# Attention on TensorE's tiles: the second half's outputs turned by 64 partitions, scores in 64x32 tiles ahead of the products within, routing groups one tile sooner

## The chip, the cores and the metric

The kernel runs on one core of a Trainium2 chip. The metric is device time in microseconds (us). TensorE (PE in the rows, PEld its weight loads) does the matmuls, VectorE (DVE), ScalarE (ACT) and GpSimd (POOL) the elementwise work, and SP issues most transfers. Each engine takes its own instructions in order.

## The reference

Three stages, in float32. First a linear attention with decay over 4 batches, 8 heads, 768 tokens, head size 32 and state size 16: within a chunk, `M = (C B^T) * L` with `L[i,j] = exp(cum_i - cum_j)` for `i >= j`, and

```
y      = M x + (C state) * exp(cum)
state  = exp(sum la) * state + sum_j B_j x_j exp(cum_last - cum_j)
```

The outputs become 3072 rows of 256. Then a mixture of 8 experts, each row to the one with the largest `x @ w_gate` (two layers of 1024 hidden units, weighted by the softmax of the gate). Then a second mixture of 4 experts, in which each row goes through all, weighted by given probabilities.

## The kernel before, in words

The attention works on 24 tiles (u) of 128 tokens, six to a batch, each in two halves (k) of 64 tokens. One loop, `for i in range(NU + 1)`, runs all stages of neighbouring tiles against each other; in it the order on every engine is the order of the calls. A turn i does, for TensorE in this order before the change:

- `scores(i+1)`: C B^T, four matmuls of 64 rows and 64 columns of weights (tile position (64q, 64k)), 256 columns each, into the PSUM tile `cb`; VectorE then multiplies by `Lt` to make `M` (L501, L503).
- `stage_c(i-1)`: two matmuls with the output `yT` of a tile as weights and a constant `rhsT` as moving operand, which is an identity with the 8 gate columns beside it. They transpose the tile back to tokens and give the gate's logits at once (L573). `store` copies both out by ScalarE (`lg`, `xo`), and SP stores `xo` to the rows `xs`.
- `decay(i+2)`: one matmul of 512 columns into `abc`, of which VectorE's scan makes `Lt` (L477, L480). In seven turns `decays_c` follows, which makes the decays of three tiles (L459).
- `within(i)`: M x, 16 matmuls in 64x32 tiles at (64k, 32h), for head pair h and half k, into `y[32h.., k]` (L515).
- `across(i)`: C state, in 32x32 tiles at (r, r) for both halves, added into the same `y` (L527). The first tile of each batch has no state for its first half. ScalarE then copies `y` to `yT` (L533).
- `gain(i+1)`: 16 matmuls of 128 rows and 32 columns into `U` (L548), of which VectorE's scan `state` makes S (L557) at the start of the next turn.

GpSimd makes `br` (`decayed_b`) and `Cs` (`decayed_c`), and splits the first expert's weights (L166). Each fp32 matmul leaves two records in the trace.

The routing of the first mixture is done in three groups of tiles, `ENDS = (12, 18, 23)`: when the turn behind a group's last tile ends, `route` puts a list of small operations into `queue`, and `slot` takes up to six of them in a turn. They find the largest logit, rank the rows by matmuls with ones and build one-hot blocks (L236) of four tiles each to invert the order. Behind the first group (EARLY) two gathers of rows for the first expert are issued, so that its first products (`ahead`) can follow the loop; the last group is routed behind the loop. `DECAYS` says in which turn each `decays_c` stands.

Of the kernel before, what the change touches and what calls it, by code (L numbers as in the profile page):

```python
# [8 lines left out]
F32 = mybir.dt.float32  # L9
# [10 lines left out]
P = 128  # L20
NB, H, S, HD, DS = 4, 8, 768, 32, 16
NT = NB * S
NCH = S // P
L = 64
NU = NT // P
D = H * HD
E1, E2, F = 8, 4, 1024
# [3 lines left out]
CAP = max(CAPS)  # L31
CAP0 = 256
GAP0 = 152
EARLY = 12
ENDS = (12, 18, 23)
NSL = 512
NC = E1 * NSL // P + 1
BIG = 3 << 29
# [5 lines left out]
def body(tc, I, out):  # L44
    nc = tc.nc
    with ExitStack() as outer:
# [266 lines left out]
        with ExitStack() as ctx:  # L313
# [98 lines left out]
            nc.gpsimd.memset(brs[0], 0.0)  # L412
            nc.vector.memset(d1, 0.0)
            nc.vector.memset(pfg[0], 0.0)
            rhsT = [ac.tile([P, P + E1], F32, name=f"rhsT{k}") for k in range(2)]
            for k in range(2):
                nc.gpsimd.tensor_copy(rhsT[k][:, (0, E1)[k]:(P, E1 + P)[k]], ident)
            select(0)
            nc.scalar.copy(delta, selF[:, None, :].broadcast_to([P, H, L]))
            select_heads(0)  # L420
# [72 lines left out]
            def scores(u):  # L493
                BT, cm = cz[u // 3 % NBC][:, 2], BC[u // 3]
                Lt = LM[u]
                M = LM[u] = sp.tile([P, H, L], F32, tag="M", name="M", bufs=2)
                cb = pa.tile([P, 2, 512], F32, tag="cb", name="cb")
                for q, k in ((0, 0), (1, 1), (0, 1), (1, 0)):
                    r = slice(64 * q, 64 * q + 64)
                    ts = slice(u % 3 * P + k * L, u % 3 * P + k * L + L)  # L500
                    nc.tensor.matmul(cb[k * L:k * L + L, q, :4 * L], BT[r, ts], cm[r, :, ts], start=True, stop=True,  # L501
                                     tile_position=(64 * q, k * L), skip_group_check=True)
                nc.vector.tensor_mul(M.rearrange("p (q h) i -> p q (h i)", q=2), cb[:, :, :4 * L],  # L503
                                     Lt.rearrange("p (q h) i -> p q (h i)", q=2))

            def within(u, q):
                b, c = divmod(u, NCH)
                if q == 0:
                    LM[u, "y"] = pa.tile([P, 2, 512], F32, tag="y", name="y", bufs=1)
                y = LM[u, "y"]  # L510
                M = LM[u]
                for h in range(4):
                    for k in range(2):
                        r = slice(k * L, k * L + L)
                        nc.tensor.matmul(y[32 * h:32 * h + 32, k, q * L:q * L + L],  # L515
                                         xb[u % NXB][r, k, (2 * h + q) * HD:(2 * h + q + 1) * HD],
                                         M[r, 2 * h + q], start=(q == 0), stop=(c == 0 and k == 0),
                                         tile_position=(k * L, 32 * h), skip_group_check=True)

            def across(u):  # L520

                b, c = divmod(u, NCH)
                LM.pop(u)
                for k in range(2):
                    if c > 0 or k > 0:
                        for r in range(0, P, 32):
                            nc.tensor.matmul(LM[u, "y"][r:r + 32, k, :P], LM[u, "S"][r:r + 32, :, k],  # L527
                                             LM[u, "Cs"][r:r + 32, :, k * L:k * L + L],
                                             start=False, stop=True, tile_position=(r, r), skip_group_check=True)

            def copy_y(u):
                yT = LM[u, "yT"] = sp.tile([P, 2, P], F32, tag="yT", name="yT")
# [3 lines left out]
            def carry(u):  # L536

                U = LM[u, "U"] = pp.tile([P, HD, 3], F32, tag="oneA", name="U")
                nc.scalar.copy(U[:, :, 0], LM[u - 1, "S"][:, :, 2] if u % NCH else zero.bitcast(F32).broadcast_to([P, HD]))
# [19 lines left out]
            def decayed_c(u):  # L559

                Cs = sp.tile([P, 2, P], F32, tag="Cs", name="Cs", bufs=2)
                nc.gpsimd.tensor_mul(Cs, cz[u // 3 % NBC][:, :2, u % 3 * P:u % 3 * P + P],
                                     PF[u // 3][:, u % 3, None, :].broadcast_to([P, 2, P]))
                LM[u, "Cs"] = Cs

            def stage_c(u):

                yT = LM.pop((u, "yT"))
                tp = pa.tile([P, 2, P + E1], F32, tag="tp", name="tp")

                flat = tp.rearrange("p k c -> p (k c)")
                for k in range(2):
                    nc.tensor.matmul(flat[:, k * P:k * P + P + E1], yT[:, k, :], rhsT[k], start=(k == 0), stop=True,  # L573
                                     skip_group_check=True)
                LM[u, "tp"] = tp

            def store(u):
# [66 lines left out]
            bc_part(2 * P, HB)  # L644
            bc_next = load_bc(1)
            bc_next[0]()
            for k in range(2):
                nc.sync.dma_start(rhsT[k][:, (P, 0)[k]:(P + E1, E1)[k]], I["wg"][k])
            load(2)
            dpr = ac.tile([P, NU, E2], F32, name="dpr")  # L650

# [39 lines left out]
            def has(u):  # L691
                return 0 <= u < NU
# [39 lines left out]
            CASTS = {**dict.fromkeys((7, 9, 11, 13, 15, 16, 17, 18, 22, 23), 1), 19: 2, 20: 2, 21: 2}  # L732
            asks = [f for t in TILES for f in load_w(0, *t, pieces=4)]
            splits = list(TILES)
            DECAYS = {max(3 * m - 2 - 2 * (m > 5), 2): m for m in range(1, NU // 3)}
            CHUNKS = {0: 3, 1: 4, 2: 2, 3: 5}
            for i in range(NU + 1):
                if i % 2 == 0 and has(i + 4):
                    load(i + 4)
                if i in stage:  # L740
                    bc = load_bc(stage[i])
                    bc[0]()
                    for k in range(2):
                        heads[3 * stage[i] - 4 + k] = [lambda h=h, bc=bc: bc[1](h) for h in range(2 * k, 2 * k + 2)]
                for f in asks[:ASKS.get(i, 0)]:
                    f()
                asks = asks[ASKS.get(i, 0):]
                if i == 6:
                    nc.sync.dma_start(dpr, I["dp"].rearrange("p (u e) -> p u e", u=NU))
                if i == 9:  # L750
                    queue += probs
                for _ in range(CASTS.get(i, 0)):
                    if not ws:
                        ws = split_w(0, *splits.pop(0), 4)
                    steps_w += [ws[:2]]
                    ws = ws[2:]
                if has(i):
                    state(i)
                slot()
                if has(i + 1):  # L760
                    if i:
                        decayed_b(i + 1)
                    scores(i + 1)
                    carry(i + 1)
                for f in soon.get(i, ()):
                    f()
                if has(i - 1):
                    stage_c(i - 1)
                slot()
                if has(i + 2):  # L770
                    decay(i + 2)
                if i in CHUNKS:
                    chunks[CHUNKS[i]]()
                if i in DECAYS:
                    decays_c(DECAYS[i])
                if has(i + 1):
                    decayed_c(i + 1)
                for fs in steps_w:
                    for f in fs:
                        f()  # L780
                steps_w = []
                if 5 <= i < 8:
                    (counts, places_first, sums_of_ones)[i - 5]()
                for f in gathers[:1]:
                    if f:
                        f()
                gathers = gathers[1:]
                slot(2)
                if i in (3, 7, 11):
                    select_heads(i // 4 + 1)  # L790
                if i % 2 == 0 and has(i + 4):
                    select(i + 4)
                if has(i - 1):
                    store(i - 1)
                if has(i):
                    within(i, 0)
                    within(i, 1)
                    across(i)
                    copy_y(i)
                for f in heads.pop(i, ()):  # L800
                    f()
                if i < 2:
                    nc.gpsimd.memset(pfg[i + 2], 0.0)
                    blank(i + 4)
                slot(2)
                if has(i + 1):
                    gain(i + 1)
                if i - 1 in GROUPS and i < NU:
                    between, after = early() if i - 1 == EARLY else ((), ())
                    queue += route(*GROUPS[i - 1], psum_a, between)  # L810
                    if after:
                        queue.append(lambda after=after: gathers.extend(after))
# [572 lines left out]
def lay_out(x, a, B, C, moe_w_gate, moe_w1, moe_w2, moe2_domain_probs, moe2_w1, moe2_w2):  # L1385
# [11 lines left out]
    au = f(a.reshape(NB, H, NCH, 2, L).transpose(0, 2, 3, 1, 4)).reshape(2 * NU, H * L)  # L1397
    au = np.concatenate([au, au[:L - 2 * NU]], 0)
    d["au"] = np.concatenate([au, au], 0)
    d["wg"] = f(moe_w_gate.reshape(4, 2, HD, E1).transpose(1, 0, 2, 3)).reshape(2, P, E1)  # L1400
    d["w1"] = f(moe_w1.reshape(E1, 4, 2, HD, F).transpose(0, 2, 1, 3, 4)).reshape(E1, D, F)
    d["w2"] = f(moe_w2)
    v1 = moe2_w1.reshape(E2, 2, P, 2, 4, P).transpose(0, 4, 2, 1, 3, 5)
# [19 lines left out]
```

## Time and profile before

| | before |
|---|---|
| three timed runs, median | 770.13 us (769.84 to 770.41) |
| the profiled execution | 769.49 us, its span 767.8 us |
| TensorE, busy | 749.9 us, 98% of the span |
| VectorE | 557.1 us, 73% |
| ScalarE | 415.2 us, 54% |
| GpSimd | 471.4 us, 61% |

The profile shows one execution. The span runs from the first to the last instruction that it records. Busy times of TensorE are of pipelined matmuls whose ends are modelled, so on TensorE the starts say more than the durations.

### The profile page before, as it was taken

To read this page: it belongs to the slowest core of one execution; us is meant where nothing else is said; L and a number is where in the kernel's file an instruction comes from. 1 tells how busy PE (TensorE), PEld (TensorE's weight loads), DVE (VectorE), ACT (ScalarE), POOL (GpSimd) and SP (SyncE) were. 2 spreads that over 40 slices of the span, in tenths; PEclk is the share of its full clock that TensorE was granted. 3 is DMA by queue.
4 is the path that set the end of the run, shared out by engine and by line. 5 is a ranking of instruction groups with operands and counts; after the bars stand their busy time and mean duration, and the time that the engine had idled before them with its cause. 6 is when DMAs were issued, how large, how long until landed. Compare 5 with 4: busy or idle time off the path is not lost.

```text
span 767.8 us, 16862 instructions
## 1 busy us (share of the span) xinstructions
PE 749.9 (98%) x6510; PEld 710.8 (93%) x6510; DVE 557.1 (73%) x988; ACT 415.2 (54%) x931; POOL 471.4 (61%) x558
## 2 busy tenths in 40 slices
PE   8999899999999999999999999999999999999994
PEld 6666798999999999999999999999999999999994
DVE  8789845664467886787966779777687887868752
ACT  7776454545455555466564555555555565454540
POOL 5557767558762854587753558765366775465544
PEclk9999999999999999999999999999999999999998
DMA  7665355434423200010000001100000100000001
GB/s 210 172 192 152 90 180 163 134 118 133 134 74 98 55 2 2 1 28 29 28 28 1 2 1 51 32 14 16 1 2 29 29 1 1 7 36 17 26 28 56
DMA packets 36146, 45.57 MB, mean 59 GB/s; under 512 B 4512, under 2 KB 26016, under 8 KB 36064
## 3 DMA queue, kind: packets, MB, share of 16 engines
q1 hardware_dynamic: 31648, 36.29, 15.9%
q0 software_dynamic: 3360, 7.13, 2.9%
q8 instruction: 52, 0.85, 0.5%
q10 hardware_dynamic: 1056, 1.05, 0.5%
q14 instruction: 30, 0.25, 0.1%
HBM read 38.12 MB, written 6.34 MB: 58 GB/s over the span
## 4 chain that ended last, share of the span: by engine, by line
PE 65%; ACT 1%; DVE 0%; POOL 0%; issue 0%; POOLq 0%; ACTq 0%; DVEq 0%
PE po L1308 35%; PE x L1242 9%; PE z L1242 9%; PE w L1242 8%; PE y L1242 4%; ACT xc L865 0%; POOL out L1328 0%; ACT s L1255 0%; DVE h L1251 0%; PE poA L1308 0%; POOLq L1419 0%; ACT h L1248 0%; DVE c L1270 0%; DVE u L1263 0%; DVE acc L1318 0%
## 5 line engine op out<-in xcount | busy, mean ns | idle before, releaser
L1308 PE MATMUL po<-w,h 128*128 128x256 f32 x2280 | 280.1, 281 | 0.3 <-DVE h L1251 0.3
L1308 PEld LDWEIGHTS po<-w,h 128*128 128x128 f32 x2280 | 277.6, 188 | 0.5 <-DVE h L1251 0.5
L1248 ACT ACTIVATE h<-c 128x384 fp32r<-128x384 f32 x192 | 98.6, 525 | 149.8 <-DVE c L1282 80.5
L1261 POOL TENSOR_TENSOR g<-s,s 128x384 f32<-128x384 f32 x64 | 65.9, 1029 | 148.2 <-ACT s L1260 147.3
L1251 DVE SCALAR_TENSOR_TENSOR h<-c,h 128x384 fp32r<-128x384 f32 x192 | 145.6, 768 | 10.9
L1263 DVE TENSOR_TENSOR u<-y,s 128x384 f32<-128x384 f32 x64 | 35.5, 555 | 68.6 <-ACT s L1260 67.0
L166 POOL TENSOR_TENSOR wl<-raw,wh 128x256 fp32r<-128x256 f32 x72 | 55.5, 798 | 36.8 <-ACT wh L160 34.3
L1242 PE MATMUL x<-xc,wh 128*128 128x384 f32 x256 | 66.9, 342 | 1.3 <-ACT s L1255 0.6
L1242 PE MATMUL w<-xc,wh 128*128 128x384 f32 x256 | 65.5, 337 | 0.0
L1242 PE MATMUL z<-xc,wh 128*128 128x384 f32 x256 | 65.4, 336 | 0.0
L1282 DVE TENSOR_TENSOR c<-u,g 128x384 f32<-128x384 f32 x63 | 58.8, 933 | 0.0
L1255 ACT COPY s<-x 128x384 f32<-128x384 f32 x64 | 30.6, 479 | 50.8 <-PE x L1242 50.8
L904 ACT ACTIVATE hh<-ph 128x216 fp32r<-128x216 f32 (+8 forms) x69 | 33.4, 489 | 43.9 <-PE ph L274 38.6
L866 POOL TENSOR_TENSOR xc<-x,xc 128x384 fp32r<-128x384 f32 x28 | 32.7, 1166 | 37.0 <-ACT xc L865 36.8
L1251 DVE SCALAR_TENSOR_TENSOR h<-x,h 128x384 fp32r<-128x384 f32 x64 | 35.7, 558 | 24.2 <-ACT h L1248 23.9
L866 POOL TENSOR_TENSOR xc<-ts,xc 128x384 fp32r<-128x384 f32 x46 | 52.3, 1151 | 0.0
L906 DVE SCALAR_TENSOR_TENSOR hl<-ph,hh 128x216 fp32r<-128x216 f32 (+8 forms) x69 | 37.2, 549 | 16.9 <-ACT hh L904 16.3
L274 PE MATMUL ph<-xh,wh 128*128 128x480 f32 (+8 forms) x142 | 48.7, 343 | 0.4 <-DVE hl L906 0.4
L925 PE MATMUL po<-hh,wh 128*128 128x480 f32 (+8 forms) x142 | 48.3, 340 | 0.0
L274 PE MATMUL ph<-xh,wl 128*128 128x480 f32 (+8 forms) x142 | 47.7, 336 | 0.0
L274 PE MATMUL ph<-xl,wh 128*128 128x480 f32 (+8 forms) x142 | 47.6, 335 | 0.0
L925 PE MATMUL po<-hl,wh 128*128 128x480 f32 (+8 forms) x142 | 47.6, 335 | 0.0
(242 smaller groups left out, 1665.1 us busy)
## 6 DMA issues: line engine op xcount, KB each, us to landing
raw<-in_w SPq DMA_DIRECT2D x26, 512.0 KB, 3.9
raw<-in_v SPq DMA_DIRECT2D x32, 256.0 KB, 2.7
xb<-in_xb SPq DMA_DIRECT2D x22, 192.0 KB, 3.8
xs<-xo SPq DMA_DIRECT2D x24, 128.0 KB, 2.6
cz<-in_cb SPq DMA_DIRECT2D x13, 192.0 KB, 3.9
raw<-in_w SPq DMA_DIRECT2D x16, 128.0 KB, 3.7
cz<-in_cb SPq DMA_DIRECT2D x2, 576.0 KB, 6.0
raw<-in_w ACTq DMA_DIRECT2D x2, 512.0 KB, 4.4
```

Of the source, the lines that this page charges most:

```text
L166: ins = nc.gpsimd.tensor_sub(lo[:, :, a:a + n], raw[:, :, a:a + n], hi[:, :, a:a + n].bitcast(F32))
L274: mm = nc.tensor.matmul(ph, w[:, k, fs], x[k], start=(i == 0), stop=(i == 5))
L866: eng.tensor_sub(o[:, 1], src, o[:, 0].bitcast(F32))
L906: i1 = nc.vector.scalar_tensor_tensor(hl, ph, 0.0, hh.bitcast(F32), op0=ALU.max, op1=ALU.subtract)
L925: mm = nc.tensor.matmul(po, w[:, f % 4, ks], h, start=(i == 0), stop=(i == 23))
L1242: nc.tensor.matmul(bank[to], w[:, a], x[:, r], start=(m == 0 and to not in seen), stop=(m == 2), skip_group_check=True)
L1248: sc.activation(HP[n][0], src, AF.Relu)
L1251: v.scalar_tensor_tensor(HP[n][1], src, 0.0, HP[n][0].bitcast(F32), op0=ALU.max, op1=ALU.subtract)
L1261: nc.gpsimd.tensor_add(g_, s5, s7)
L1263: v.tensor_add(u2, bank["y"], s1)
L1282: v.tensor_add(c22, u2, g_)
L1308: nc.tensor.matmul(two[h], x[:, ts], w2[:, w, j], start=(i, j, h * (len(hs) - 1), m) == (0, 0, 0, 0), stop=(i, j, m) == (3, 1, 2), skip_gr ...
```

## The change

- `within` and `across` write the second half (k = 1) to the output partitions turned by 64: `o = (32h + 64k) % 128`. So the two halves of a matmul pair no longer use the same column group of the array; in `across` the tiles are (r, r) and (r, r + 64).
- `scores` makes eight matmuls of 32 columns of weights instead of four of 64, 256 columns each.
- `stage_c` undoes the turn: four matmuls in place of two, each with 64 tokens of `yT` as weights, in 128x64 tiles; the second half uses a turned identity and turned gate weights. The constant is one tile `turned`; the gate's part comes by one transfer instead of two and is spread into it by two GpSimd copies (`turn_in`) in turn 0. The host's layout gives the gate weights in both orders.
- In the loop `decay(i+2)` comes first, then `stage_c`, `decays_c`, and `scores(i+1)` directly ahead of `within(i)`; before, `scores` came first. The chunk products that stood behind `decay` now stand behind `scores`.
- The routing groups end one tile sooner, (11, 17, 23): 12, 6 and 6 tiles in place of 13, 6 and 5. `EARLY` is 11. The sixth and seventh `decays_c` come two turns later.

```
-EARLY = 12
-ENDS = (12, 18, 23)
+EARLY = 11
+ENDS = (11, 17, 23)
...
+            turned = ac.tile([P, 2, P + 2 * E1], F32, name="turned")
+            nc.gpsimd.tensor_copy(turned[:, 0, E1:E1 + P], ident)
+            for o in (0, L):
+                nc.gpsimd.tensor_copy(turned[:, 1, E1 + o:E1 + o + L], ident[:, L - o:P - o])
...
-                    nc.tensor.matmul(cb[k * L:k * L + L, q, :4 * L], BT[r, ts], cm[r, :, ts], start=True, stop=True,
-                                     tile_position=(64 * q, k * L), skip_group_check=True)
+                    for j in (0, 32):
+                        o = k * L + j
+                        js = slice(ts.start + j, ts.start + j + 32)
+                        nc.tensor.matmul(cb[o:o + 32, q, :4 * L], BT[r, js], cm[r, :, ts], start=True, stop=True,
+                                         tile_position=(64 * q, o), skip_group_check=True)
...
-                        nc.tensor.matmul(y[32 * h:32 * h + 32, k, q * L:q * L + L],
+                        o = (32 * h + k * L) % P
+                        nc.tensor.matmul(y[o:o + 32, k, q * L:q * L + L],
...
-                            nc.tensor.matmul(LM[u, "y"][r:r + 32, k, :P], LM[u, "S"][r:r + 32, :, k],
+                            o = (r + k * L) % P
+                            nc.tensor.matmul(LM[u, "y"][o:o + 32, k, :P], LM[u, "S"][r:r + 32, :, k],
                                              LM[u, "Cs"][r:r + 32, :, k * L:k * L + L],
-                                             start=False, stop=True, tile_position=(r, r), skip_group_check=True)
+                                             start=False, stop=True, tile_position=(r, o), skip_group_check=True)
...
-                for k in range(2):
-                    nc.tensor.matmul(flat[:, k * P:k * P + P + E1], yT[:, k, :], rhsT[k], start=(k == 0), stop=True,
-                                     skip_group_check=True)
+                n = P + E1
+                for q in range(2):
+                    for k in range(2):
+                        ts = slice(k * L, k * L + L)
+                        nc.tensor.matmul(flat[ts, q * P:q * P + n], yT[:, q, ts], turned[:, k, E1 - q * E1:E1 - q * E1 + n],
+                                         start=(q == 0), stop=True, tile_position=(0, k * L), skip_group_check=True)
...
+            wgt = ac.tile([P, 2, 2 * E1], F32, name="wgt")
+            nc.sync.dma_start(wgt, I["wg"])
+            def turn_in():
+                for q in range(2):
+                    nc.gpsimd.tensor_copy(turned[:, :, (P + E1, 0)[q]:(P + 2 * E1, E1)[q]],
+                                          wgt[:, q].rearrange("p (k e) -> p k e", k=2))
...
-            DECAYS = {max(3 * m - 2 - 2 * (m > 5), 2): m for m in range(1, NU // 3)}
+            DECAYS = {max(3 * m - 2, 2): m for m in range(1, NU // 3)}
...
-                    scores(i + 1)
                     carry(i + 1)
+                if has(i + 2):
+                    decay(i + 2)
                 for f in soon.get(i, ()):
                     f()
                 if has(i - 1):
                     stage_c(i - 1)
                 slot()
-                if has(i + 2):
-                    decay(i + 2)
-                if i in CHUNKS:
-                    chunks[CHUNKS[i]]()
                 if i in DECAYS:
                     decays_c(DECAYS[i])
                 if has(i + 1):
+                    scores(i + 1)
+                if i in CHUNKS:
+                    chunks[CHUNKS[i]]()
+                if has(i + 1):
                     decayed_c(i + 1)
+                if not i:
+                    turn_in()
```

## Rows read from the trace of the kernel before

**Rows 1.** The page: busy time by engine; chain that ended last, by line.

```profile
PE 749.9 (98%) x6510; PEld 710.8 (93%) x6510; DVE 557.1 (73%) x988; ACT 415.2 (54%) x931; POOL 471.4 (61%) x558
...
PE po L1308 35%; PE x L1242 9%; PE z L1242 9%; PE w L1242 8%; PE y L1242 4%; ACT xc L865 0%; POOL out L1328 0%; ACT s L1255 0%; DVE h L1251 0%; PE poA L1308 0%; POOLq L1419 0%; ACT h L1248 0%; DVE c L1270 0%; DVE u L1263 0%; DVE acc L1318 0%
```

**Rows 2.** Waits of TensorE, 84-250 us, then 250-768: total, times, longest (us).

```profile
PE ip L250 <- DVE om L236: 0.5, 1, 0.5
...
PE x L1242 <- ACT s L1255: 0.6, 1, 0.6
```

**Rows 3.** Stretches: length; busy us (count) PE, PEld, DVE, ACT, POOL; clock; DMA; GB/s.

```profile
40.00:48.00 8.00, 8.00 (x220) 5.12 (x216) 6.13 (x9) 5.84 (x22) 4.27 (x8) 1.00 0.73 199
...
64.00:72.00 8.00, 6.61 (x169) 4.17 (x170) 7.88 (x15) 5.57 (x19) 6.39 (x10) 1.00 0.57 156
```

**Rows 4.** Timeline of one turn: start, us, engine, line, operation.

```profile
36.75 0.66 PE L501 MATMUL cb<-cm,cz 64*64 64x256 f32 x8
...
37.34 0.73 PE L573 MATMUL tp<-rhsT,yT 128*128 128x136 f32 x4
...
37.48 0.69 DVE L503 TENSOR_TENSOR M<-cb,Lt 128x512 f32<-128x512 f32 x1
...
37.83 0.48 PE L477 MATMUL abc<-ah,pk 128*128 128x512 f32 x1
...
38.24 0.45 PE L515 MATMUL y<-M,xb 64*32 64x64 f32 x32
...
38.42 1.22 DVE L480 TENSOR_TENSOR_SCAN Lt<-abc,delta 128x512 f32<-128x512 f32 x1 [0.24 <-PE abc L477]
...
38.62 0.66 PE L527 MATMUL y<-Cs,S 32*32 32x128 f32 x16
...
39.21 0.27 PEld L548 LDWEIGHTS U<-xb,br 128*32 128x32 f32 x16 [0.19 <-issue]
39.21 0.43 PE L548 MATMUL U<-xb,br 128*32 128x64 f32 x16
39.35 0.37 ACT L533 COPY yT<-y 128x256 f32<-128x256 f32 x1 [0.66 <-PE y L527]
...
39.57 0.66 PE L501 MATMUL cb<-cm,cz 64*64 64x256 f32 x8
```

**Rows 5.** Timeline: the state's products of a batch's first tile, and what follows.

```profile
66.64 0.43 PE L527 MATMUL y<-Cs,S 32*32 32x128 f32 x8 [0.81 <-DVE S L557]
...
67.00 0.43 PE L548 MATMUL U<-xb,br 128*32 128x64 f32 x16
```

**Rows 6.** Timeline of the first turns: GpSimd, and TensorE's first transposes.

```profile
6.21 0.19 POOL L398 COPY spare<-spare 64x6 f32<-64x6 f32 x1 [3.01 <-DVE spare L397]
...
12.80 0.70 PE L573 MATMUL tp<-rhsT,yT 128*128 128x136 f32 x4
...
13.01 0.73 POOL L562 TENSOR_TENSOR Cs<-cz,pf 128x256 f32<-128x256 f32 x1
...
14.71 0.41 POOL L488 TENSOR_TENSOR br<-xb,Lt 128x128 f32<-128x128 f32 x1
...
15.53 0.66 PE L501 MATMUL cb<-cm,cz 64*64 64x256 f32 x8
```

**Rows 7.** Timeline of VectorE: the scans S of turns 13, 14; last group's first reduction.

```profile
48.38 0.35 DVE L557 TENSOR_TENSOR_SCAN S<-pfg,U 128x96 f32<-128x96 f32 x1
...
51.55 0.35 DVE L557 TENSOR_TENSOR_SCAN S<-pfg,U 128x96 f32<-128x96 f32 x1 [0.50 <-ACT xo L582]
...
84.28 0.19 DVE L626 TENSOR_REDUCE top<-lg 128x5 f32<-128x40 f32 x1
```

**Rows 8.** Timeline of VectorE: one-hot blocks of the first and second group.

```profile
64.19 2.04 DVE L236 TENSOR_TENSOR om<-iota,m 128x512 f16<-128x512 f16 x2
...
69.02 0.26 DVE L236 TENSOR_TENSOR om<-iota,m 128x128 f16<-128x128 f16 x1
...
82.84 1.03 DVE L236 TENSOR_TENSOR om<-iota,m 128x512 f16<-128x512 f16 x2
```

More of the change, by code (lines that the diff above doesn't have):

```diff
@@ L414, in body @@
             nc.vector.memset(pfg[0], 0.0)
-            rhsT = [ac.tile([P, P + E1], F32, name=f"rhsT{k}") for k in range(2)]
-            for k in range(2):
-                nc.gpsimd.tensor_copy(rhsT[k][:, (0, E1)[k]:(P, E1 + P)[k]], ident)
+            turned = ac.tile([P, 2, P + 2 * E1], F32, name="turned")
+            nc.gpsimd.tensor_copy(turned[:, 0, E1:E1 + P], ident)
+            for o in (0, L):
+                nc.gpsimd.tensor_copy(turned[:, 1, E1 + o:E1 + o + L], ident[:, L - o:P - o])
             select(0)
@@ L514, in within @@
                         r = slice(k * L, k * L + L)
-                        nc.tensor.matmul(y[32 * h:32 * h + 32, k, q * L:q * L + L],
+                        o = (32 * h + k * L) % P
+                        nc.tensor.matmul(y[o:o + 32, k, q * L:q * L + L],
                                          xb[u % NXB][r, k, (2 * h + q) * HD:(2 * h + q + 1) * HD],
                                          M[r, 2 * h + q], start=(q == 0), stop=(c == 0 and k == 0),
-                                         tile_position=(k * L, 32 * h), skip_group_check=True)
+                                         tile_position=(k * L, o), skip_group_check=True)
             def across(u):
@@ L571, in stage_c @@
                 flat = tp.rearrange("p k c -> p (k c)")
-                for k in range(2):
-                    nc.tensor.matmul(flat[:, k * P:k * P + P + E1], yT[:, k, :], rhsT[k], start=(k == 0), stop=True,
-                                     skip_group_check=True)
+                n = P + E1
[4 more added lines that the diff above has]
+                                         start=(q == 0), stop=True, tile_position=(0, k * L), skip_group_check=True)
                 LM[u, "tp"] = tp
@@ L646, in body @@
             bc_next[0]()
-            for k in range(2):
-                nc.sync.dma_start(rhsT[k][:, (P, 0)[k]:(P + E1, E1)[k]], I["wg"][k])
+            wgt = ac.tile([P, 2, 2 * E1], F32, name="wgt")
[4 more added lines that the diff above has]
+                                          wgt[:, q].rearrange("p (k e) -> p k e", k=2))
             load(2)
@@ L1399, in lay_out @@
     d["au"] = np.concatenate([au, au], 0)
-    d["wg"] = f(moe_w_gate.reshape(4, 2, HD, E1).transpose(1, 0, 2, 3)).reshape(2, P, E1)
+    wg = moe_w_gate.reshape(4, 2, HD, E1).transpose(0, 2, 1, 3).reshape(P, 2, E1)
+    d["wg"] = f(np.stack([wg, np.roll(wg, L, 0)], 2)).reshape(P, 2, 2 * E1)
     d["w1"] = f(moe_w1.reshape(E1, 4, 2, HD, F).transpose(0, 2, 1, 3, 4)).reshape(E1, D, F)
```

## The prediction

> **What bounds the kernel now.** I read the page's first lines and its chain of waits first [rows 1]. TensorE is busy for 98% of the span, and the lines of the chain that ended last that have a share above 1% (35 + 9 + 9 + 8 + 4, so 65% of the span) are the second mixture's products; no line of the attention is among them. That says nothing yet on a change in attention, so next I read what TensorE waited for, by stretch [rows 2]: from 84 us to 250 us no wait sums to more than 0.5 us, from 250 us on to no more than 0.6 us. So from about 92 us on TensorE is fed without a pause, and whatever time the attention ends sooner or later moves the end by the same amount. The change has to be priced in the first 90 us, by when the last routing group can start.
>
> There the view by stretches [rows 3] separates two regimes. At 40 to 48 us TensorE is busy for all 8.00 us and VectorE for 6.13; at 64 to 72 us VectorE is busy for 7.88 of 8 and TensorE falls to 6.61. [...] So TensorE sets the pace of the early turns of the loop, VectorE that of the late ones, where the routing groups' small operations lie in its queue.
>
> **One turn where TensorE paces.** The timeline of one turn [rows 4] gives the starts: scores 36.75, transposes 37.34, decay 37.83, within 38.24, across 38.62, gain 39.21, next scores 39.57. The intervals are 0.59, 0.49, 0.41, 0.38, 0.59, 0.36: a turn of 2.82 us. How an interval is made up is seen where a sequence has no carried state [rows 5]: there across has 8 records instead of 16 (each matmul leaves two) and takes 0.36 (66.64 to 67.00) instead of 0.59. So two more rounds of 128 columns on the same four tiles cost 0.23, a round 0.115 (0.9 ns a column and record), and what is left, 0.36 - 0.23 = 0.13, is the change to the next tile shape. By this rule (0.9 ns times columns times rounds, plus about 0.15 at a change of shape) scores, on four 64x64 tiles, give 2 x 0.22 + 0.15 = 0.59; within, on eight 64x32 tiles, 4 x 0.055 + 0.16 = 0.38; gain, on four 128x32 tiles, 4 x 0.055 + 0.14 = 0.36; the transposes 4 x 0.12 with no change of shape before decay. All agree with the row. So tiles at different places do run side by side, up to eight of them, two to four to a row group.
>
> **The change, part by part.**
> *Across.* The second half's tiles move two column groups away, so both halves have tiles of their own: 16 records on eight tiles are two rounds, 0.36 instead of 0.59: -0.23 a turn. In four of the 24 tiles (0, 6, 12, 18) the first half has no state, and nothing is won. Bounds: 0.36 [rows 5] and 0.59 [rows 4]; I take 0.36, as within shows eight tiles at once.
> *Scores.* 16 records on eight 64x32 tiles are again two rounds of 256, 0.44; within has the same shape, so the change between them goes: -0.15. Bounds 0.44, and 0.88 if only four run at once.
> *Transposes.* Eight records on two 128x64 tiles: four rounds of 136, 0.47, as now; but a shape of their own puts a change behind decay and one behind them: about +0.13. Bounds 0.47 if the change to it is free, and 8 x 0.12 + 0.15 = 1.1 if the two tiles don't run together; I take 0.62, because gain, also 128 rows deep, runs its four column tiles together [rows 4].
> New turn: decay 0.41, transposes 0.62, scores 0.44, within 0.38, across 0.36, gain 0.36 = 2.57, so -0.25, or about -0.22 with something left to dependencies. The nearest of these: the transposes wait for ScalarE's copy yT, which ends at 39.72 [rows 4]; behind gain and decay they would now want it at 39.21 + 0.36 + 0.41 = 39.98, so 0.26 us is left of a cover that was 0.44. In turns in which ScalarE also copies the chunk decays it may cost 0.1. VectorE's order turns to S, Lt, M (0.35 + 1.22 + 0.69 = 2.26 [rows 4, 7]), which fits into 2.57; M is wanted a turn later.
>
> [...]
>
> *First turns.* The gate's columns now come through a tile that GpSimd spreads in turn 0, behind its Cs product, which ends at 13.74 [rows 6]. Two small copies (0.19 us is the nearest one) end at about 14.15, while the first transposes started at 12.80. From 14.2 on: 0.62 + 0.44 + 0.38 + 0.36 + 0.36 ends turn 1 at 16.36, against 15.53 before: +0.83. GpSimd's own br, 14.71 before, comes at 15.1 and is in time. Turns 2 and 3 win 0.22 each, so turn 4 starts +0.4 late. Bounds: 0, if the copies find GpSimd free early, and 1.0. The third copy into the constant lies in GpSimd's 3.01 us of idleness [rows 6] and SP issues one transfer less (0.43 us): nothing.
> *Turns 4 to 12.* Seven of the nine win 0.22 (not 6 and 12): -1.5. Turn 13 then starts at 0.4 - 1.5 = -1.1.
> *Routing one tile sooner.* Now the first group's operations begin in the turn whose S starts at 51.55, and from there VectorE is nearly without a gap until the last group's first reduction at 84.28 [rows 7]: 32.73 us for ten turns, groups one and two, and the end of the loop. After the change they begin a turn sooner, at 48.38 - 1.1 = 47.3. The same work lies ahead, less 0.4 (a group of 12 makes three one-hot blocks, not four: the odd one was 0.26 [rows 8], and shorter rows), but 11 turns. The extra turn costs between VectorE's own 2.05 (its three operations less their overlaps) and TensorE's 2.57: I take 2.3. So the last group starts at 47.3 + 32.73 - 0.4 + 2.3 = 81.9 instead of 84.28: -2.4. It has six tiles instead of five, some ten operations that each grow by about 0.01 and one more rank matmul: +0.1. The early gathers go a turn sooner with the groups. Two turns get the rank matmuls between scores and within, two changes of shape of 0.15 each, where VectorE paces: nothing. Two of the decays_c move behind, to turns that VectorE paces: nothing.
>
> **Sum.** -1.1 - 1.3 + 0.1 = -2.3 us. The profiled execution took 769.49 us around its span of 767.8, so its like would take 767.2. The median of the three timed runs, 770.13, lies 0.64 above it; on that the forecast is 767.8. Its own range, from a turn's 0.1 to 0.35 over seven turns, the startup's 0 to 1.0 and the extra turn's 2.05 to 2.6, is 766.3 to 769.3.
>
> **Rivals.**
> *Slower: the transposes' two tiles queue.* If a 128x64 tile's stream waits for its neighbour's, the step takes 1.1 instead of 0.62: +0.47 in each of the turns 2 to 12 and some 0.4 in the four late ones that TensorE paces, 5.2 + 1.6 = +6.8, and with -2.3 the result is +4.5: 774.6. It decides from about +0.16 a turn on. [...] Against it: gain's four 128x32 tiles [rows 4]. Chance 0.13.
> *Nothing to be seen.* Either across keeps its 0.59 because the two streams of a row group collide (then -0.8 is left), or the sooner routing only shifts VectorE's work against GpSimd's weight splits, with which it shares time late (two one-hot blocks took 2.04 together [rows 8] and the second group's two 1.03), and only the -1.1 of the early turns is left: 769.1 either way. Chance 0.24.
> *More.* If the change from 128x128 to 128x64 is free, nine more turns win 0.15, and if the spreading copies are early, 0.4: 767.8 - 1.8 = 766.0. Chance 0.15. The forecast itself has 0.48.
>
> A measurement of this kernel tells about 0.2% (1.5 us) from no change. Faster by more than that are nearly all of the forecast's case (0.41), the larger gain (0.15) and a little of the second rival (0.04): 0.60. Slower: the first rival and a little for what I don't see: 0.15. The same: 0.25. The range runs from 765.6, below the larger gain, to 771.2, above the no-change case; outside are the slower rival and some tails.
>
> **What would show it.** Right: across to gain 0.36 in the timeline, scores to within 0.44, transposes to scores 0.6, a turn of 2.6 at 36 to 48 us, the last group's first reduction near 82 us, TensorE without waits behind 92 us. A first transpose that waits for GpSimd until about 14.2 shows the startup's price. Wrong: transposes to scores at 0.9 or more, across still at 0.59, or VectorE's stretch ending at 84 us although turn 13 starts a microsecond sooner.

## The result, and the profile after

The changed kernel takes 775.45 us (median of six runs, 773.85 to 778.27), the kernel before 770.27 us beside it: ratio 1.0068, interval 1.0047 to 1.0089. It is slower by some 5.2 us; 767.8 was forecast, and the range ended at 771.2. Its profiled execution took 773.95 us around a span of 772.2, 4.4 us more than the span of before. It is the second shortest of the six, so its trace shows somewhat less of the loss than the median.

The page's first lines look as before [rows 1]: TensorE is busy for 97% of the span.

```profile
PE 751.3 (97%) x6798; PEld 712.9 (92%) x6798; DVE 558.3 (72%) x987; ACT 415.0 (54%) x931; POOL 471.6 (61%) x561
```

The waits of TensorE from 84 to 250 us (in total, times, longest) have one new entry at their head, 1.6 us for the one-hot blocks; it is at the very start of that window. Behind it nothing sums to more than 0.5 us, so what the attention loses goes to the end one to one, as in [rows 2].

```profile
PE ip L250 <- DVE om L236: 1.9, 2, 1.6
PE ip L250 <- ACT hx L265: 0.5, 1, 0.5
```

The start of VectorE's state scan S marks a turn in each kernel. This table, from the timelines of VectorE, says where the time went (us; "first reduction" and "indices" are the last group's):

| kernel | S turn 3 | S turn 13 | S turn 22 | S turn 23 | first reduction | indices |
|---|---|---|---|---|---|---|
| before | 19.38 | 48.38 | 77.22 | 81.07 | 84.28 | 89.42 |
| after | 20.24 | 49.84 | 80.18 | 84.42 | 87.55 | 94.05 |
| difference | +0.86 | +1.46 | +2.96 | +3.35 | +3.27 | +4.63 |

The forecast had -1.1 at turn 13 and -2.4 at the first reduction. So all three stretches went wrong: the early turns lost 1.5 instead of winning 1.1, the routing stretch lost another 1.8 instead of winning 1.3, and the last group took 1.4 longer.

**An early turn.** TensorE's timeline of one turn after (start, us), to hold against [rows 4]:

```profile
35.02 0.50 PE L478 MATMUL abc<-ah,pk 128*128 128x512 f32 x1
35.44 0.68 PE L582 MATMUL tp<-turned,yT 128*64 128x136 f32 x8
36.06 0.66 PE L505 MATMUL cb<-cm,cz 64*32 64x256 f32 x16
36.51 0.59 PE L520 MATMUL y<-M,xb 64*32 64x64 f32 x32
37.03 0.46 PE L533 MATMUL y<-Cs,S 32*32 32x128 f32 x16
37.43 0.43 PE L554 MATMUL U<-xb,br 128*32 128x64 f32 x16
37.79 0.50 PE L478 MATMUL abc<-ah,pk 128*128 128x512 f32 x1
```

The starts are 0.42, 0.62, 0.45, 0.52, 0.40 and 0.36 apart: a turn of 2.77 us against 2.82. The transposes take the 0.62 that was forecast, across 0.40 instead of 0.59 (0.36 was forecast), scores the 0.45 (0.44). But within takes 0.52 where it took 0.38, so scores and within together are 0.97 as before (0.59 + 0.38). The weight loads of within take longer too; first a turn after, then the turn of before that [rows 4] show:

```profile
36.30 0.64 PEld L520 LDWEIGHTS y<-M,xb 64*32 64x32 f32 x32
```

```profile
38.24 0.29 PEld L515 LDWEIGHTS y<-M,xb 64*32 64x32 f32 x32 [0.25 <-PE tp L573]
```

**The first turns.** TensorE's first transposes wait for GpSimd's copies, and turn 1 ends at 16.42 (16.36 was forecast):

```profile
14.08 0.68 PE L582 MATMUL tp<-turned,yT 128*64 128x136 f32 x8 [1.26 <-POOL turned L661]
...
16.42 0.50 PE L478 MATMUL abc<-ah,pk 128*128 128x512 f32 x1
```

**The end of the loop.** VectorE's timeline after, from S of turn 22 to the last group's first reduction:

```profile
80.18 0.34 DVE L563 TENSOR_TENSOR_SCAN S<-pfg,U 128x96 f32<-128x96 f32 x1
...
81.00 0.68 DVE L507 TENSOR_TENSOR M<-cb,Lt 128x512 f32<-128x512 f32 x1
81.60 2.89 DVE L236 TENSOR_TENSOR om<-iota,m 128x512 f16<-128x512 f16 x2
84.42 0.34 DVE L563 TENSOR_TENSOR_SCAN S<-pfg,U 128x96 f32<-128x96 f32 x1
84.81 0.19 DVE L629 TENSOR_TENSOR idxf<-idxf,ip 128x33 f32<-128x33 f32 x1
87.55 0.20 DVE L635 TENSOR_REDUCE top<-lg 128x6 f32<-128x48 f32 x1 [2.56 <-ACT lg L590]
```

The reader is to see three things. The second group's two one-hot blocks take 2.89 us, 1.03 before [rows 8]. They now stand ahead of the last S; before, they stood behind it (82.84 against 81.07). And from 84.81 + 0.19 to 87.55 VectorE has nothing to do: 2.56 us, waiting for the last tile's logits. Before, that stretch (81.07 to 84.28) was where the second group's last operations lay, and the first reduction followed them without a gap. On TensorE the blocks' matmuls wait, ahead of the last tile's products:

```profile
81.98 0.68 PE L582 MATMUL tp<-turned,yT 128*64 128x136 f32 x8
84.22 0.55 PE L250 MATMUL ip<-ot,om 128*128 128x33 f16 x6 [1.55 <-DVE om L236]
84.70 0.45 PE L520 MATMUL y<-M,xb 64*32 64x64 f32 x32
85.08 0.46 PE L533 MATMUL y<-Cs,S 32*32 32x128 f32 x16
85.48 0.20 PE L621 MATMUL rk<-before,ones_b 128*128 128x56 bf16 x1
86.13 1.17 PE L582 MATMUL tp<-turned,yT 128*64 128x136 f32 x8 [0.46 <-ACT yT L539]
```

The last transposes take 1.17 where the ones before them took 0.68: the granted clock has fallen. By stretches (columns as in [rows 3]; the clock is the third number from the end):

```profile
80.00:88.00 8.00, 4.77 (x107) 3.32 (x108) 5.36 (x11) 2.73 (x11) 4.15 (x7) 0.85 0.19 52
88.00:96.00 8.00, 6.77 (x55) 5.88 (x53) 7.40 (x27) 3.39 (x10) 3.81 (x5) 0.93 0.06 18
```

By stretches of 1 us the clock reads 1.00 from 80 to 85 us, 0.82 from 85 to 86, 0.50 in each of the three from 86 to 89, 0.97 from 89 to 90 and 1.00 behind that. The fall, at 85.6, comes 1.4 us behind the end of TensorE's 1.55 us wait (84.22). Before, both stretches had 1.00, with TensorE busy for 6.32 and 7.32.

### The profile page after: what moved, and what is told of

Read it like the earlier page. It is cut to its first block, busy times and chain, and to the rows that moved or that the text cites. A ratio compares the mean times of both kernels' runs of the same rounds, so it can differ in the third digit from the quotient of the medians.

```text
span 772.2 us, 17430 instructions
## 1 busy us (share of the span) xinstructions
PE 751.3 (97%) x6798; PEld 712.9 (92%) x6798; DVE 558.3 (72%) x987; ACT 415.0 (54%) x931; POOL 471.6 (61%) x561
## 4 chain that ended last, share of the span: by engine, by line
PE 65%; ACT 1%; DVE 0%; POOL 0%; issue 0%; POOLq 0%; ACTq 0%; DVEq 0%
PE po L1326 35%; PE x L1260 9%; PE z L1260 8%; PE w L1260 8%; PE y L1260 4%; ACT xc L883 0%; POOL out L1346 0%; ACT s L1273 0%; DVE h L1269 0%; PE poA L1326 0%; POOLq L1438 0%; ACT h L1266 0%; DVE c L1288 0%; DVE u L1281 0%; DVE acc L1336 0%
```

## The experiments

All twelve kernels in one table, each against the kernel before on its chip:

| run | what it is | ratio | 95% interval |
|---|---|---|---|
| e1 | after, routing as before | 1.0024 | 1.0013 to 1.0035 |
| e2 | before, routing one tile sooner | 1.0036 | 1.0024 to 1.0048 |
| e3 | after, gate columns without GpSimd | 1.0078 | 1.0056 to 1.0101 |
| e4 | e1 and e3 together | 1.0032 | 1.0018 to 1.0047 |
| e5 | after, scores in 64x64 tiles | 1.0045 | 1.0028 to 1.0062 |
| e7 | after, two weight splits later | 1.0024 | 1.0013 to 1.0036 |
| e8 | after, TensorE kept busy at the wait | 1.0033 | 1.0020 to 1.0045 |
| e9 | before, scores in 64x32 tiles | 1.0006 | 0.9997 to 1.0016 |
| e10 | after, blocks behind the last S | 1.0021 | 1.0008 to 1.0035 |
| e11 | before, two weight splits later | 0.9999 | 0.9982 to 1.0016 |
| e12 | after with e3, e5, e7 and e10 | 1.0012 | 0.9996 to 1.0027 |
| e13 | e2 with e7 and e10 | 1.0009 | 0.9995 to 1.0024 |

**e1 and e2: the two halves of the change.**

```
-EARLY = 11
-ENDS = (11, 17, 23)
+EARLY = 12
+ENDS = (12, 18, 23)
```

So in e1, from after; e2 makes the opposite edit in the kernel before. The table DECAYS goes with it each time.

> The changed kernel with the routing groups put back to (12, 18, 23) and the two late decays to their old turns; the turned tiles, the new order of the loop and the spreading copies stay. In the changed trace S of turn 13 comes 1.5 us later than before, and another 2.9 us are lost between there and the first mixture. Theory A (the sooner groups cost the 2.9 us, because the second group's one-hot blocks now stand ahead of the last S and its matmul ahead of the last products within): about 1.5 us over before, some 771.8. Rival B (the tiles and the new order cost it all along, the sooner groups win the 1.2 us that was forecast): 776 or more, slower than the changed kernel.

> The kernel before with only the routing groups one tile sooner (11, 17, 23) and the two late decays two turns later. Theory A: 2.5 to 3 us slower than before, about 773, with the two one-hot blocks of the second group at 1.4 us each beside GpSimd's weight splits and TensorE's clock below 1.00 behind them. Rival B: 1.2 us faster than before, 769.

Measured: 773.37 and 774.61 us; +0.24% and +0.36% add up to 0.60%, near the whole change's 0.68%. Neither half is a gain. In e1 turn 13's S starts at 50.30, and from there to turn 23's takes 32.65 us, as before (32.69): the turned tiles cost time early and change nothing where VectorE paces. In e2 turn 13's S is near its old place (48.97), and from there to turn 23's takes 34.47 us. (Some 0.5 us of what both are late at turn 13 is there at the first S already: 10.53 and 10.57, before 10.04.) So e2 shows the routing's loss alone, and the same picture as after, with a granted clock of 0.67 from 80 to 88 us and another operation held, m for 2.33 us:

```profile
80.13 2.33 DVE L254 SCALAR_TENSOR_TENSOR m<-t,sl 128x6 f16<-128x6 f32 x1
82.50 1.03 DVE L236 TENSOR_TENSOR om<-iota,m 128x512 f16<-128x512 f16 x2
83.44 0.35 DVE L557 TENSOR_TENSOR_SCAN S<-pfg,U 128x96 f32<-128x96 f32 x1
83.86 0.19 DVE L620 TENSOR_TENSOR idxf<-idxf,ip 128x33 f32<-128x33 f32 x1
87.50 0.20 DVE L626 TENSOR_REDUCE top<-lg 128x6 f32<-128x48 f32 x1 [3.44 <-ACT lg L581]
```

**e3 and e4: the early turns without the wait for GpSimd.**

```
-            wgt = ac.tile([P, 2, 2 * E1], F32, name="wgt")
-            nc.sync.dma_start(wgt, I["wg"])
+            for q in range(2):
+                nc.sync.dma_start(turned[:, :, (P + E1, 0)[q]:(P + 2 * E1, E1)[q]],
+                                  I["wg"][:, q].rearrange("p (k e) -> p k e", k=2))
...
-                if not i:
-                    turn_in()
```

> The changed kernel with the gate's columns written by two transfers straight into the constant, without GpSimd's spreading copies. If the first transposes' wait for these copies (1.26 us in the changed trace) is a loss that stays to the end, 0.8 us less than the changed kernel. If the early turns catch it up, or something else holds turn 2 back, no difference.

> The first and the third together: old groups, gate's columns by transfer, turned tiles and new order stay. Theory A: within 0.7 us of before, as a turn of the changed kernel has 2.77 us on TensorE where nothing waits, against 2.82. Rival B: 3 us or more over before, as every turn pays for the 128x64 tiles.

Measured: 777.36 and 774.57 us, no better than their partners. In e3 turn 3's S does come sooner (19.62 instead of 20.24), but turn 13's starts at 49.95, later than after's. What ate it in this execution are idle times of TensorE inside a sequence for which the profile names no releaser ("issue"), 0.17, 0.60 and 0.29 us in e3 by then, 0.71 and 0.60 in e4. The kernel before has none in these turns. In e4 the granted clock falls as well, to 0.61 from 88 to 96 us, although the routing is the old one; why is open, and e4 is no clean price of the turned tiles.

**e5 and e9: the scores' tiles alone.**

```
-                    for j in (0, 32):
-                        o = k * L + j
-                        js = slice(ts.start + j, ts.start + j + 32)
-                        nc.tensor.matmul(cb[o:o + 32, q, :4 * L], BT[r, js], cm[r, :, ts], start=True, stop=True,
-                                         tile_position=(64 * q, o), skip_group_check=True)
+                    nc.tensor.matmul(cb[k * L:k * L + L, q, :4 * L], BT[r, ts], cm[r, :, ts], start=True, stop=True,
+                                     tile_position=(64 * q, k * L), skip_group_check=True)
```

(e5 from after; e9 makes the opposite edit in the kernel before.)

> The changed kernel with scores in four 64x64 tiles again, in the new place directly ahead of the products within. In the changed trace scores and within together take 0.97 us from start to start, as before (0.59 + 0.38), so the change of shape seems to have been worth nothing. Theory A (no drain was saved, and the eight records and eight weight loads more a turn cost something through stalls in which TensorE waits for nothing that the profile shows): the two together still 0.97, fewer such stalls, 0.5 to 1.3 us less than the changed kernel. Rival B (0.15 a turn was saved): 0.15 x 22 = 3 us more.

> The kernel before with scores in eight 64x32 tiles, in their old place. Theory A (a larger number of TensorE instructions a turn brings stalls in which it waits for nothing shown): such stalls of 0.2 to 0.8 us appear in the loop, 0.5 to 2 us over before. Rival B (the stalls come from the new order or from the 128x64 shape): no such stalls, within 0.3 us of before.

Measured: 773.18 and 770.85 us. In e5's turn scores take 0.59 and within 0.39 again, 0.98 together:

```profile
37.89 0.68 PE L579 MATMUL tp<-turned,yT 128*64 128x136 f32 x8
38.50 0.66 PE L502 MATMUL cb<-cm,cz 64*64 64x256 f32 x8
39.09 0.45 PE L517 MATMUL y<-M,xb 64*32 64x64 f32 x32
39.48 0.46 PE L530 MATMUL y<-Cs,S 32*32 32x128 f32 x16
39.87 0.43 PE L551 MATMUL U<-xb,br 128*32 128x64 f32 x16
40.23 0.50 PE L478 MATMUL abc<-ah,pk 128*128 128x512 f32 x1
```

So the 64x32 tiles are worth nothing in a turn: 2.77 us either way. What becomes of the saving is seen in e9. There the same tiles have the transposes, of another shape, behind them, and take 0.60:

```profile
40.99 0.66 PE L504 MATMUL cb<-cm,cz 64*32 64x256 f32 x16
41.59 0.73 PE L576 MATMUL tp<-rhsT,yT 128*128 128x136 f32 x4
```

In the changed kernel, with within's like shape behind them, they take 0.45. So their own interval does lose 0.15; within gives it back. e5 has no stall in the early turns; its turn 13 starts at 49.11, turn 3 at 20.23, 28.88 us for ten turns against 29.00 before. So without stalls the turned products and the new order win 0.12 us in ten turns. In time e5 lies below after, but the intervals overlap, and e9, where the same tiles cost at most 0.16%, shows two stalls in its profiled execution, the larger of them

```profile
21.74 0.42 PE L518 MATMUL y<-M,xb 64*32 64x64 f32 x21 [0.63 <-issue]
```

All eight kernels with the 64x32 scores have such stalls in their profiled execution; but so have two of the six without them (e11: 0.28 and 0.43; e12: 0.81 and 0.52), at other times each. The traces say what they have in common. Number all of TensorE's records in the trace from the first on, matmuls, weight loads and semaphore records together: all 24 such stalls above 0.1 us from 8 to 62 us, in ten kernels, lie at record 193 or 194 or a multiple of 256 behind it, and each ends 1.26 to 1.61 us after a transfer of 16 KB has landed on DMA queue 8, which the page lists as of kind "instruction". In the changed kernel they are records 1474 (34.03 us) and 1730 (38.46 us), each 1.43 us after such a transfer landed (32.60 and 37.03); its queue 8 makes 54 of them for 13708 records, about one for every 256. That the stalls are waits for TensorE's own instructions is the author's estimate from these numbers; no edit tested it. Most such places pass without a stall (11 or 12 up to 62 us in each kernel). The kernels with the 64x32 scores, whose turn has 16 matmul and load records more for the scores, have 19 of the 24.

**e7, e8 and e11: what holds the blocks, and what the clock adds.** e7 and e11 move the weight splits of turns 22 and 23, which GpSimd makes behind a cast by ScalarE, to turn 24, the loop's last, in after and in before; e8 puts seven matmuls whose result nobody reads into TensorE's order ahead of the 1.55 us wait.

```
-            CASTS = {**dict.fromkeys((7, 9, 11, 13, 15, 16, 17, 18, 22, 23), 1), 19: 2, 20: 2, 21: 2}
+            CASTS = {**dict.fromkeys((7, 9, 11, 13, 15, 16, 17, 18), 1), 19: 2, 20: 2, 21: 2, 24: 2}
```

```
+                if i == NU - 1:
+                    w = psum_a([P, P], "filler")
+                    for _ in range(7):
+                        nc.tensor.matmul(w, ident, ident, start=True, stop=True)
                 slot(2)
```

> The changed kernel with the weight splits of turns 22 and 23 (one each on ScalarE and GpSimd) put into turn 24. Theory A (the second group's one-hot blocks, 2.89 us, last so long because GpSimd works beside them; TensorE waits for them ahead of the last products within): blocks 1.0 to 1.8 us, TensorE's gap of 1.55 us ahead of the group's matmul below 0.6, clock above 0.95 from 80 to 88 us, 1.5 to 3 us less than the changed kernel. Rival B (the blocks are slow by themselves, or the splits come back on the path of the first expert): no change, or slower.

> The changed kernel with seven matmuls (14 records) of identity by identity, whose output nobody reads, between the transposes of turn 23 and the second group's matmul, where TensorE stands idle for 1.55 us. If the clock below 1.00 from 80 to 96 us comes from this gap and costs time behind it: clock 1.00 there, the last transposes 0.7 instead of 1.17 us, 0.7 to 1.0 us less than the changed kernel. If the clock falls anyway or the stretch waits for VectorE, no difference.

> The kernel before with GpSimd's weight splits of turns 22 and 23 moved to turn 24, the edit that took about 0.4% off the changed kernel. Theory A (that edit undid a collision which the sooner routing had made: in the kernel before the second group's blocks already run behind the last S in 1.03 us): ratio 0.999 to 1.001. Rival (the late splits are a gain of their own, whatever the routing): ratio 0.996 to 0.997, and the fastest kernel so far.

Measured: 771.47, 772.45 and 771.97 us. With the splits out of the way the blocks take 1.54 instead of 2.89 us and TensorE's wait for them is 0.20; the last S follows the one before it by 2.89 us instead of 4.24, and the clock stays at 1.00:

```profile
81.94 1.54 DVE L236 TENSOR_TENSOR om<-iota,m 128x512 f16<-128x512 f16 x2
83.40 0.34 DVE L563 TENSOR_TENSOR_SCAN S<-pfg,U 128x96 f32<-128x96 f32 x1
83.78 0.19 DVE L629 TENSOR_TENSOR idxf<-idxf,ip 128x33 f32<-128x33 f32 x1
86.04 0.20 DVE L635 TENSOR_REDUCE top<-lg 128x6 f32<-128x48 f32 x1 [2.07 <-ACT lg L590]
```

In the kernel before the same edit gives nothing (0.9999): it undid a collision that the sooner routing had made. e8 leaves the blocks at 2.90 us, but from 80 to 96 us its clock is 1.00, the last transposes take 0.68, and the last S is followed by the first reduction in 2.64 us instead of 3.13. So a part of the loss is the clock that falls behind TensorE's idle time. How large it is stays uncertain: the ratios (0.33% against 0.68%) say half, 2.7 us, but their intervals only just part, while in the two traces the way from the last S to the indices is 8.72 instead of 9.63 us, 0.9 us. That the clock falls is no chance of one execution. Its mean over a whole execution is 0.986 to 0.994 in every execution of the four kernels with sooner groups that leave this wait as it is (after, e2, e3, e5), and 0.995 to 0.997 in seven of the eight of e8 and six of the seven of e7.

**e10 and e13: the blocks' place.** Three empty entries in the second group's list put its blocks behind the last S, and their matmuls and the end of the list behind the last transposes.

```
-                    + hots + [None, None, None, mm, None] + [lambda: finish(o["ip"])])
+                    + [None] * (3 * (g0 == ENDS[0] + 1)) + hots + [None, None, None, mm, None] + [lambda: finish(o["ip"])])
```

> The changed kernel with one thing moved: the second group's two one-hot blocks stand on VectorE behind the last state scan S instead of ahead of it, and their six matmuls on TensorE behind the last transposes. Theory A (the sooner routing loses because the second group's blocks, held beside GpSimd's splits for 2.89 us, stand in front of the last S, while afterwards VectorE waits 2.56 us for the last logits with nothing to do): the last S moves from 84.42 to about 82.2, the last group's first reduction from 87.55 to about 85.5, TensorE's wait of 1.55 for the blocks goes and the granted clock stays at 1.00 from 80 to 96 us; the time is 1.5 to 2.5 us below the changed kernel's, ratio to the kernel before 1.004. Theory B (it doesn't matter where the blocks stand, they are long because GpSimd works beside them): the last S comes sooner, the first reduction doesn't, ratio 1.006 to 1.007.

> The kernel before with the routing groups one tile sooner, the second group's blocks behind the last S, and the splits of turns 22 and 23 in turn 24. Theory A: from turn 13 to the last S 33 us as in the kernel before (32.69), the last group has six tiles instead of five, ratio 0.9995 to 1.0015. Rival (a sooner routing wins its 1.2 us once nothing stands in front of the last S): ratio 0.998.

Measured: 773.39 and 772.51 us. e10 takes 0.47% off the changed kernel, more than its theory asked. VectorE's timeline of e10:

```profile
80.53 0.35 DVE L563 TENSOR_TENSOR_SCAN S<-pfg,U 128x96 f32<-128x96 f32 x1
...
82.69 0.35 DVE L563 TENSOR_TENSOR_SCAN S<-pfg,U 128x96 f32<-128x96 f32 x1 [0.67 <-ACT yT L539]
82.96 1.89 DVE L236 TENSOR_TENSOR om<-iota,m 128x512 f16<-128x512 f16 x2
85.68 0.19 DVE L629 TENSOR_TENSOR idxf<-idxf,ip 128x33 f32<-128x33 f32 x1 [0.82 <-PE ip L250]
85.78 0.20 DVE L635 TENSOR_REDUCE top<-lg 128x6 f32<-128x48 f32 x1
```

The last S comes 2.16 us behind the one before it instead of 4.24. The blocks are still held (1.89), but now in the time that the last tile's products take anyway, and the first reduction follows 0.93 us behind them, of which 0.82 is a wait for their matmuls. The clock is 1.00 throughout, and TensorE is busy for 6.52 us where it was 4.77:

```profile
80.00:88.00 8.00, 6.52 (x162) 4.55 (x147) 6.30 (x20) 3.58 (x13) 4.77 (x8) 1.00 0.26 69
88.00:96.00 8.00, 7.09 (x61) 6.61 (x60) 6.72 (x24) 3.90 (x11) 6.12 (x6) 1.00 0.31 97
```

The indices come at 90.94, 3.1 us sooner than after, but the span is only 1.1 us shorter. Most of the other 2.0 us goes between 93 and 126 us, where TensorE now waits for the first expert's operands: 1.3 us for VectorE's `hl`, 0.4 for its `xl` and 0.3 for ScalarE's `xh`; after has 0.2 for `hl` there.

e13 asks what a sooner routing is worth when nothing stands in front of the last S: 1.0009, no gain. From its last S to the first reduction are 3.06 us (80.74 to 83.80), before 3.21; turn 13's S to the first reduction takes 35.14 us, before 35.90, and e11, with the old routing, also 35.14. The indices come at 89.53, before at 89.42, so nothing is won there. Yet e13's span is 1.8 us longer, most of it by the same waits behind the indices as in e10, so its ratio doesn't price the routing alone.

**e12: all costs out.**

> The changed kernel with every cost found so far taken out: scores in four 64x64 tiles (no stalls of TensorE for instructions), the gate's columns straight from memory (no wait for GpSimd's copies in turn 1), the second group's blocks behind the last S, the splits of turns 22 and 23 in turn 24. Theory A (turned products and the new order leave a turn of 2.78 us against 2.82, and routing one tile sooner can't bring the last group forward, which waits for the last tile): turn 13's S at 48.2 to 48.6, the last group's first reduction at 84 to 85, ratio 0.999 to 1.001. Rival (the turned products do win 0.2 us a turn, hidden by those costs): S of turn 13 at about 47, ratio 0.997.

Measured: 772.91 us, 1.0012. Its undisturbed turns are 2.77 us, but two stalls of 0.81 and 0.52 put turn 13's S at 51.26, where 48.2 to 48.6 was expected: that part missed. So the first reduction is late too, at 86.28 instead of 84 to 85. The stretch from turn 13's S to it, 35.02 us, is no longer than expected, with 2.97 from the last S (83.31) and the clock at 1.00. No kernel beats the one before.

## Why the prediction was wrong, step by step

*Transposes, across, first turns: right.* 0.62, 0.40 (0.36 forecast) and a turn 1 that ends at 16.42 (16.36). The rival that the two 128x64 tiles queue is refuted: at 1.1 us they would show in every turn. That its 774.6 lies near the measured time is chance.

*Scores, -0.15: failed, in the next term.* "Within has the same shape, so the change between them goes" came true for the scores (0.45 against 0.60 in e9), but the sum kept within at 0.38, and it took 0.52. After, e5 and before give 0.97, 0.98 and 0.97 for the pair, with and without a change between them. That a change of shape costs some 0.15 by itself (what e5's expectation calls a drain) was the author's estimate from [rows 4] and [rows 5]; by that alone the pair would have become shorter, and it did not. What the row shows is that within's loads take 0.64 instead of 0.29; why is open.

*A turn 0.22 shorter: failed.* With within at 0.52 and across at 0.40 it is 2.77, so 0.05 shorter, and over ten turns 0.12 us were left (e5). In turns 6 and 12, which begin a batch, the forecast had "nothing is won"; they lose 0.14 and 0.15 (e5 2.75, before 2.61 and 2.60), for there the transposes' price stands without a gain in across. With the startup's 0.86 and stalled turns (turn 8's S comes 3.49 us behind turn 7's, 3.17 before) the forecast -1.1 at turn 13 became +1.46. e1 prices this half at +0.24%, 1.8 us.

*Routing sooner, -1.3: failed, and the larger part.* "The same work lies ahead, less 0.4, but 11 turns" took VectorE as the bound up to the last group's first reduction, since it had no gap there [rows 7]. From turn 13's S to that reduction 34.6 us were forecast (47.3 to 81.9); 37.71 were measured. What the last group waits for is the last tile: S, across, copy, transposes and logits, 3.2 us before and 3.1 after. VectorE had no gap only because the second group's rest lay in these 3.1 us. Sooner routing pulled that rest in front of the last S, where it delays what the last group waits for, and left the 3.1 us empty: VectorE is busy for 34.01 us of the 37.5 from the first group's reduction to the last's, before 30.62 of 32.5. Of the 3.4 us more, the extra turn's three operations are 2.1, as forecast; 1.4 are one-hot blocks held beside GpSimd. By the ratios e10, which moves the blocks, gives back 0.47%, and e7, which takes GpSimd's work from beside them, 0.44%; the two overlap. With both, the sooner routing in the kernel before takes 1.0009 (e13) instead of 1.0036 (e2). The rival "nothing to be seen" had named this sharing of time, but not the place in the order that makes it count.

*What follows on TensorE* stood in no step: 1.55 us of idleness and a granted clock of 0.85, then 0.93. e8 shows that filling it wins back 0.9 us by the traces, 0.35% by the ratios.

*The last group, +0.1: failed, for a reason of its own.* From its first reduction to the indices it took 6.50 us instead of 5.14. But e10, also with six tiles, takes 5.16, and e11 and e9, with five, 6.46 and 6.05. So the sixth tile is not the cause. Here too VectorE is held beside GpSimd, in the second of the last group's blocks and in the operation `pb` behind it; after:

```profile
91.43 1.55 DVE L236 TENSOR_TENSOR om<-iota,m 128x512 f16<-128x512 f16 x2
92.67 0.91 POOL L266 TENSOR_TENSOR hl<-hx,hh 128x256 fp32r<-128x256 f32 x1
92.91 0.75 DVE L990 TENSOR_TENSOR pb<-at,nth 128x64 f32<-128x64 f32 x1
```

The second block takes 0.95 of the 1.55, and `pb` 0.75; in e10 they take 0.42 and 0.22. That is 1.07 of the 1.36 us; e11 and e9 show the same (`pb` 0.76 and 0.75). Why e10 differs there is open.

*One to one to the end: right for this change.* +4.63 us at the indices, +4.4 in the span. It is no rule: from the indices to the end are 678.4 us before and 678.2 after, but 680.1 to 680.2 in e10, e12 and e13, where TensorE has the waits told above.

## What to carry to other kernels

An engine without gaps in front of a late step need not be what that step waits for: look for the chain that the step's own data needs, and ask which work only fills the wait. Work that is moved sooner is put in front of something; find what stands behind it in each engine's order, and whether another engine works beside it there (here two blocks of 1.03 us took up to 2.89). What one interval on TensorE loses, the next can take (here scores went from 0.59 to 0.45, within from 0.38 to 0.52): a saved change of tile shape is priced by a row with two neighbours of one shape, and by both of their intervals together.

## What the runs showed of the hardware

The first of the two one-hot blocks in the changed kernel takes 2.56 us, before 0.69; the second 0.41, before 0.42. GpSimd's timeline beside it, in the changed kernel:

```profile
81.52 0.73 POOL L568 TENSOR_TENSOR Cs<-cz,pf 128x256 f32<-128x256 f32 x1
82.21 1.40 POOL L166 TENSOR_TENSOR wl<-raw,wh 128x256 fp32r<-128x256 f32 x2
```

The first block starts at 81.60, when GpSimd has just begun, and ends at 84.16, 0.55 us behind the end of GpSimd's run (82.21 + 1.40 = 83.61). In the kernel before, at 82.84, no GpSimd instruction runs beside it (one ends at 82.77, the next starts at 83.60), and it takes 0.69: so by estimate some 0.55 of its 0.69 us of work lie behind the three GpSimd instructions. In e10 the run ends at 83.96 and the held block at 84.52, again 0.56 later. In e7, where of the three only `Cs` runs beside it (81.85 to 82.58), it takes 1.20 and ends at 83.14, 0.56 later too. M, which reads one operand from PSUM, takes 0.68 at 81.00 although GpSimd works then as well (0.42 us from 81.14), and 0.69 in [rows 4]. Why the block is held and M is not, no run shows. Nor is it the same everywhere: from 91.43 the first of the last group's blocks takes 0.68 while GpSimd's `la` (91.39 to 92.70) runs; the second takes 0.95 and ends at 92.99, while `hl` (92.67 to 93.58) runs.

TensorE's stalls without a releaser, 0.12 to 0.82 us each, come in ten of the fourteen kernels, at some of the records 193 or 194 plus a multiple of 256, and can cost an early turn a quarter of its time (e1: 0.71 us at 46.99, where a turn without a stall takes 2.77). An edit worth 0.1 us a turn can't be told beside them from one profiled execution.
